# Gate/up chunks on 64-row halves, and the first numerators moved behind them, in a gated mix of linear attention and a gated feed-forward

## The chip, the cores and the metric

The kernel runs on one core of a Trainium2 chip. The metric is the device time of one execution in microseconds (us); the lower the better.

## The reference

A sequence of 2048 tokens of width 640 goes through two branches. Branch A is linear attention with 32 heads of 20 features, where the softmax of the projected features and of their negatives takes the place of the attention softmax. Branch B is a feed-forward block of width 1728 with a gelu gate. A sigmoid per token mixes them.

```python
g = sigmoid((x * gate_w).sum(-1, keepdims=True))
q, k, v = split_heads(x @ wqkv)                    # 32 heads of 20
phi = lambda z: concat([softmax(z @ w_phi), softmax(-(z @ w_phi))])
kv, z = phi(k).T @ v, phi(k).sum(tokens)           # per head
o = (phi(q) @ kv) / (phi(q) @ z + 1e-6)
a = merge_heads(o) @ wo
b = (gelu(x @ w_gate) * (x @ w_up)) @ w_down
out = g * a + (1 - g) * b
```

## The kernel before

The program is written by hand, and a small layer (`_Sched`) puts in the semaphore waits. Each operation names what it reads and writes, and a write waits for the last reader of each engine. The PSUM banks are named `("ps", 0)` to `("ps", 7)`; each holds 128 x 512 fp32 numbers. Operations run on each engine in the order in which the Python code issues them.

The stages in order:

- `attention_state`: the projections, the exponentials of keys and queries, and the sums over tokens (`gram`, L637) that become the small matrices `KV`. It ends about 80 us into the span.
- Gate/up, four blocks of 512 tokens (`gateups`). A block has 14 chunks of the width 1728, in the order 0, 1, 13, 2 to 12; chunk 13 is the narrow remainder. `gateup` issues for a chunk five full-height matmuls (128 rows, 512 columns, L464) for the gate into one bank and five for up into the next, then gelu on ScalarE (L779) from the gate bank, and the product with the up bank on VectorE (L781). The products stay in SBUF as `hT`. Chunks take turns on the bank pairs (0, 1) and (6, 7).
- Down, the same four blocks (`downs`). `down_pair` makes two tiles of 128 tokens: 64-row matmuls (L898), two at a time, one on the upper half of the rows into one tile's bank and one on the lower half into the other's; in the second half of the work ("closing") the halves change banks. Each `yield` of it is one such pair, called a step here; there are 148 in a block, 74 for each two tiles, of which 38 are opening. The last five of every pass multiply the attention output `goT` with `wo`. The banks are again (0, 1) and (6, 7).
- Between these, the attention output of each 128 tokens, called a numerator here (`num`, tile t = 0 to 15). `num_mms` issues 22 matmuls of 64 rows and 66 columns (L817), two at a time, into four banks: two for each of the two signs. `num_steps` issues eleven VectorE operations: a reciprocal from the banks (L851), seven more small ones, two wide multiplies from the banks (L863) to O1 and O2, and their sum (L866) to Og. A DMA transpose (L869, SP queue) brings Og to `goT`. All of VectorE's operations that read banks name all four of them.

In the down stage the numerators use banks 2 to 5, and their places are given in steps of the block:

```python
at = (1, 31, 61, 91)
for b in range(self.NB):
    downs(b, {at[k]: 4 * b + 2 + k for k in range(4 if b < 3 else 2)})
```

Numerators 0 and 1 are needed by the first two tiles of the down stage, and so come earlier: in block 1 of gate/up, behind its fifth chunk. `num_pair` issues their 44 matmuls in one go into banks 2 to 7, and `first_nums` deals out the VectorE steps between the products of the next chunks, which use other bank pairs meanwhile.

Of the kernel before, what the change touches and what calls it, by code (L numbers as in the profile page):

```python
# [3 lines left out]
P = 128  # L4
BF16 = mybir.dt.bfloat16
F32 = mybir.dt.float32
AF = mybir.ActivationFunctionType
ALU = mybir.AluOpType
# [99 lines left out]
class _Kernel:  # L108
    S, D, H, DH, F = 2048, 640, 32, 20, 1728
    KD = D // P  # L110
# [7 lines left out]
    DB = DH + 2  # L118
# [641 lines left out]
    def gateup(self, b, c, banks):  # L760
        sc = self.sc
        xs = lambda kt: self.xT[:, kt, b * self.BT:(b + 1) * self.BT]
        xr = [("xT", t) for t in range(4 * b, 4 * b + 4)]
        old = (self.oldw, self.oldk, self.oldq, [("xT", t) for t in range(12)])[b]
        hT, hk = self.hT(b, c), b
        slot = self.gn % 3
        self.gn += 1
        if c < 13:
            i = 0 if c < 7 else 1
            early = c in self.UP + self.LATE  # L770
            done = early and b == 0
            if done:
                banks = banks[::-1]
            for w, wk, bk in ((self.wg_sb, "wg", banks[0]), (self.wu_sb, "wu", banks[1]))[:1 if done else 2]:
                for kt in range(self.KD):
                    key = self.upheld(c)[1] if early and wk == "wu" else (wk, i, kt)
                    self.mm(bk, 0, 512, w[:, kt, c * P:(c + 1) * P], xs(kt), kt == 0, kt == self.KD - 1, xr + [key])
            up, upk = (self.upheld(c)[0], ("upf", c)) if done else (self.bank(banks[1]), ("ps", banks[1]))
            sc.op("act", lambda e: e.activation(self.gl[:, slot, :], self.bank(banks[0]), AF.Gelu_apprx_tanh),  # L779
                  reads=[("ps", banks[0])], writes=[("gl", slot)], guard=self.oldw)  # L780
            sc.op("dve", lambda e: e.tensor_tensor(hT, up, self.gl[:, slot, :], ALU.mult),  # L781
                  reads=[upk, ("gl", slot)], writes=[("hT", hk, c)], guard=old)
        else:
            bk = banks[0]
            for kt in range(self.KD):
                self.mm(bk, 0, 512, self.wgu_sb[:, kt, :], xs(kt), kt == 0, kt == self.KD - 1, xr + ["wgu0", "wgu1"])
            sc.op("act", lambda e: e.activation(self.gl[64:128, slot, :], self.ps[0:64, bk * 512:bk * 512 + 512],
                                                AF.Gelu_apprx_tanh),
                  reads=[("ps", bk)], writes=[("gl", slot)], guard=self.oldw)
            for r in (0, 1):  # L790
                odd = lambda v: v.rearrange("p (u r q) -> p u r q", r=2, q=P)[:, :, r, :]
                sc.op("dve", lambda e: e.tensor_tensor(
                    odd(hT[64 * r:64 * r + 64, :]), odd(self.ps[64:128, bk * 512:bk * 512 + 512]),
                    odd(self.gl[64:128, slot, :]), ALU.mult),
                    reads=[("ps", bk), ("gl", slot)], writes=[("hT", hk, c, r)], guard=old)

    def before_num(self):
        return ([("upf", c) for c in self.UP + self.LATE] + ["kstage", "qstage"] + [("wref", k, h) for k in (0, 3) for h in (0, self.HM)] + [("wref", k, 0) for k in (1, 2, 4)] + [("xtok", k) for k in range(4)] + ["wkT", "wqT"])

    def num(self, t):  # L800
        NBK, DB, old = self.NUMB, self.DB, self.before_num()
        w = self.HG * DB
        base = [(NBK + 2 * s) * 512 + 512 - 6 * w for s in (0, 1)]
        self.num_mms(t, base, 0)
        rb = [("ps", NBK + k) for k in range(4)]
        for step in self.num_steps(t, base, rb, old):
            step()

    def num_mms(self, t, base, late):
        sc, w = self.sc, self.HG * self.DB  # L810
        for g in range(self.G):
            n = min(w, self.H * self.DB - w * g)
            for s in (0, 1):
                a, o = 64 * s, base[s] + w * g
                edge = o // 512 != (o + w) // 512
                first = g == 0 or (o - w) // 512 != o // 512
                sc.op("pe", lambda e: e.matmul(  # L817
                    self.ps[:, o:o + n], self.Eq[a:a + 64, g, t * P:(t + 1) * P], self.KV[a:a + 64, g, 0:n],
                    start=first and not (late and g == 0), stop=edge or g == self.G - 1, skip_group_check=True),
                    reads=[("Eq", t), "KVd", ("KV", 0), ("KV", 8), ("KV", 10)], writes=[("ps", o // 512)],  # L820
                    signal=edge or g == self.G - 1)

    def num_pair(self):
        w = self.HG * self.DB
        top = 512 - 6 * w
        over = 512 + 512 - 3 * w
        bases = [[(2 + 3 * s) * 512 + c for s in (0, 1)] for c in (top, over)]
        rb = [("ps", b) for b in range(2, 8)]
        steps = []
        for t in (0, 1):  # L830
            self.num_mms(t, bases[t], t)
        for t in (0, 1):
            n = {0: (0, 1, 3, 4), 1: (1, 2, 4, 5)}[t]
            steps.append(self.num_steps(t, bases[t], [rb[k] for k in n], self.before_num()))
        return steps

    def num_steps(self, t, base, rb, old):
        sc = self.sc
        DB, DH, H = self.DB, self.DH, self.H
        sl = t % 2  # L840
# [2 lines left out]
        Dn = [v[:, :, DH + 1] for v in V]  # L843
        R = lambda k: self.RH[:, sl, k, :]
        key = lambda k: ("RH", sl, k)
        small, wide, fin = [], [], []
        into = small

        def dve(fn, reads, writes, guard=()):
            into.append(lambda: sc.op("dve", fn, reads=reads, writes=writes, guard=guard))  # L850
        dve(lambda e: e.reciprocal(R(0), Dn[1]), rb, [key(0)], guard=old)  # L851
        dve(lambda e: e.tensor_tensor(R(1), Dn[0], R(0), ALU.mult), rb + [key(0)], [key(1)])
        dve(lambda e: e.tensor_tensor(R(2), Z[1], R(1), ALU.mult), rb + [key(1)], [key(2)])
# [2 lines left out]
        dve(lambda e: e.reciprocal(R(5), R(4)), [key(4)], [key(5)])  # L856
        dve(lambda e: e.tensor_scalar(R(6), R(5), self.Gr[:, t:t + 1], None, op0=ALU.mult), [key(5), "Gr"], [key(6)])
        dve(lambda e: e.tensor_tensor(R(7), R(6), R(1), ALU.mult), [key(6), key(1)], [key(7)])
        into = wide
        for s, dst in ((0, self.O1), (1, self.O2)):  # L860
            o = dst[:, sl, :].rearrange("p (h d) -> p h d", d=DH)
            f = R(6 + s).unsqueeze(2).to_broadcast([P, H, DH])
            dve(lambda e, o=o, f=f, s=s: e.tensor_tensor(o, V[s][:, :, 0:DH], f, ALU.mult),  # L863
                rb + [key(6 + s)], [("O", s, sl)], guard=old)
        into = fin
        dve(lambda e: e.tensor_tensor(self.Og[:, sl, :], self.O1[:, sl, :], self.O2[:, sl, :], ALU.add),  # L866
            [("O", 0, sl), ("O", 1, sl)], [("Og", sl)], guard=old)
        gs = t % 8
        fin.append(lambda: sc.dma("sp", lambda e: e.dma_start_transpose(self.goT[:, gs, :, :], self.Og[:, sl, :]),  # L869
                                  reads=[("Og", sl)], writes=[("goT", gs)], guard=old))  # L870

        def run(part):
            for f in part:
                f()
        return [lambda p=p: run(p) for p in (small, wide, fin)]

    def down_pair(self, t0, banks, widths):

# [60 lines left out]
                    evac(h)  # L939
                yield None  # L940

    NUMB = 2
    oldk = [("Ek", k, s) for k in range(5) for s in (0, 1)] + [(w, k) for w in ("Ekc", "Ekp") for k in range(5)] + [
        (w, k) for w in ("vaug", "vmain", "vone") for k in range(9)]
    oldq = [("Eqt", k, s) for k in range(4) for s in (0, 1)] + [(w, k) for w in ("Eqtc", "Eqtp") for k in range(4)] + [
# [3 lines left out]
    def ffn(self):  # L949
        self.gn = 0  # L950
        self.pn = 0
        pairs = [(0, 1), (6, 7)]

        def gateups(b, after, other={}):
            for idx, c in enumerate([0, 1, 13] + list(range(2, 13))):
                self.gateup(b, c, other.get(idx, pairs[self.pn % 2]))
                self.pn += 1
                after(idx)

        def downs(b, side):  # L960
            p = [pairs[(self.pn + k) % 2] for k in (0, 1)]
            n = 0
            for t in (4 * b, 4 * b + 2):
                final = t + 2 == self.NT
                for _ in self.down_pair(t, p + [(2, 3)] if final else p, (256, 256, 128) if final else (320, 320)):
                    n += 1
                    if n in side:
                        self.num(side[n])

        def state(idx):  # L970
            if idx < 4:
                self.gram(12 + idx)
            if idx == 3:
                self.kv_state()
                self.gates()

        left = []

        def first_nums(idx):
            if idx == 4:  # L980
                left.extend(f for steps in self.num_pair() for f in steps)
            for _ in range({4: 1, 5: 1, 6: 2, 7: 1, 8: 1}.get(idx, 0)):
                left.pop(0)()

        def none(idx):
            pass
        at = (1, 31, 61, 91)
        gateups(0, state)
        gateups(1, first_nums, {k: ((0, 1), (0, 1), (0, 5), (1, 2))[k - 5 if k < 7 else 2 + (k - 7) % 2]
                                for k in range(5, 14)})  # L990
        gateups(2, none)
        gateups(3, none)
        for b in range(self.NB):
            downs(b, {at[k]: 4 * b + 2 + k for k in range(4 if b < 3 else 2)})

# [43 lines left out]
```

## Time and profile before

| What | Value |
|---|---|
| Time, median of 3 runs | 283.51 us (283.3 to 283.77) |
| Span of the profiled execution | 282.4 us |
| Around the span (median less span; the profiled execution has no other time of its own) | about 1.1 us |
| TensorE matmuls busy | 278.6 us, 99% |
| VectorE, ScalarE busy | 173.2 us (61%), 105.9 us (38%) |
| Granted TensorE clock | 1.000 |
| Gate/up blocks | about 80 to 194.8 us |
| Down stage | 194.8 to 280.4 us |

The span runs from the first to the last instruction. In the timeline a line gives the start, the busy time, the engine, the line of the program, the operation and its operands; a bracket gives the idle time before it and what ended it. PE is TensorE's matmuls, PEld its weight loads, DVE is VectorE, ACT ScalarE. [...]

### The profile page before, as it was taken

The page shows a single profiled execution, that of the slowest core. Times are in us where ns is not written, and L with a number is a line of the kernel's source. Part 1 is how long each engine was busy: PE and PEld are TensorE (multiplying, and loading weights), DVE is VectorE, ACT ScalarE, POOL GpSimd, SP SyncE. Part 2 cuts the span into 40 slices and gives each one's busy share as a digit, 9 for nine tenths or more (in the row PEclk, how much of TensorE's full clock was granted, in tenths as well). Part 3 has the DMA queues.
Part 4 walks back from the last instruction along what each step waited for, and adds up shares of the span by engine and source line. Part 5 has one row for each costly group of instructions (what it writes and reads, how often), then busy time and mean ns, then how long its engine had stood idle before and what let it go on. Part 6 is the DMA issues. An engine that isn't in the chain of part 4 may idle for free.

```text
span 282.4 us, 6904 instructions
## 1 busy us (share of the span) xinstructions
PE 278.6 (99%) x2926; PEld 168.6 (60%) x2926; DVE 173.2 (61%) x329; ACT 105.9 (38%) x204; POOL 15.1 (5%) x69
## 2 busy tenths in 40 slices
PE   7999999999999999999999999999999999999996
PEld 4566766665665444444444444445777777777786
DVE  1456999999997523694333324235883883883801
ACT  3246978777793332223232232321112112112011
POOL 7511001101000000000000000000000000000000
PEclk9999999999999999999999999999999999999999
DMA  7999169787789910011000000000133132532221
GB/s 213 193 223 190 29 127 172 153 175 149 157 175 274 350 51 0 2 24 23 2 0 0 0 2 0 0 0 2 26 50 98 46 49 78 66 49 73 73 72 49
DMA packets 60378, 24.11 MB, mean 85 GB/s; under 512 B 51002, under 2 KB 59834, under 8 KB 60346
## 3 DMA queue, kind: packets, MB, share of 16 engines
q1 hardware_dynamic: 59680, 23.63, 38.9%
q8 instruction: 23, 0.38, 0.6%
q10 hardware_dynamic: 666, 0.03, 0.2%
q14 instruction: 9, 0.07, 0.1%
HBM read 9.04 MB, written 2.62 MB: 41 GB/s over the span
## 4 chain that ended last, share of the span: by engine, by line
PE 97%; DMA 1%; SPq 0%; ACT 0%; issue 0%
PE ps L464 58%; PE ps L898 29%; PE ps L599 4%; PE ps L817 2%; PE ps L478 2%; PE ps L637 2%; DMA w<-in_A_wqkv_dram 1%; PE ps L404 1%; SPq L230 0%; SPq L251 0%; ACT outsb L911 0%; PE ps L370 0%
## 5 line engine op out<-in xcount | busy, mean ns | idle before, releaser
L464 PE MATMUL ps<-xT,wu_sb 128*128 128x512 bf16 x260 | 64.1, 379 | 0.0
L464 PE MATMUL ps<-xT,wg_sb 128*128 128x512 bf16 x260 | 63.9, 379 | 0.0
L779 ACT ACTIVATE gl<-ps 128x512 bf16<-128x512 f32 x52 | 31.0, 597 | 70.3 <-PE ps L464 70.3
L464 PE MATMUL ps<-w,xT 128*128 128x362 bf16 (+5 forms) x340 | 51.4, 302 | 0.0
L898 PE MATMUL ps<-wd_sb,hT 64*128 64x320 bf16 x648 | 48.4, 296 | 0.0
L781 DVE TENSOR_TENSOR hT<-ps,gl 128x512 bf16<-128x512 f32 x34 | 23.4, 689 | 37.7 <-PE ps L464 37.7
L464 PEld LDWEIGHTS ps<-xT,wu_sb 128*128 128x128 bf16 x260 | 25.4, 98 | 30.3 <-DVE hT L781 0.2
L464 PEld LDWEIGHTS ps<-xT,wg_sb 128*128 128x128 bf16 x260 | 25.1, 98 | 29.8 <-issue 0.2
L911 ACT ACTIVATE outsb<-ps,Gm 128x320 bf16<-128x320 f32 (+2 forms) x31 | 14.5, 515 | 71.8 <-PE ps L898 71.8
L464 PEld LDWEIGHTS ps<-w,xT 128*128 128x128 bf16 x340 | 31.9, 97 | 14.8
L898 PEld LDWEIGHTS ps<-wd_sb,hT 64*128 64x128 bf16 x648 | 30.9, 94 | 12.2 <-issue 0.4
L898 PE MATMUL ps<-wo_sb,goT 64*128 64x320 bf16 (+2 forms) x340 | 26.5, 288 | 0.0
L617 DVE TENSOR_REDUCE Dk<-Ek 128x66 f32<-128x1320 bf16 x16 | 24.3, 1520 | 2.3 <-ACT gcol L528 2.3
L626 DVE TENSOR_TENSOR Ek<-Ek,Dk 128x1320 bf16<-128x1320 bf16 x16 | 24.5, 1532 | 0.5
L863 DVE TENSOR_TENSOR O<-ps,RH 128x640 bf16<-128x640 f32 x32 | 24.7, 815 | 0.0
L538 ACT ACTIVATE Ek<-ps 128x627 bf16<-128x627 f32 x32 | 20.5, 693 | 6.4 <-PE ps L599 4.9
L538 ACT ACTIVATE Eqt<-ps 128x627 bf16<-128x627 f32 x32 | 20.6, 705 | 2.5 <-PE ps L464 2.5
L781 DVE TENSOR_TENSOR xT<-ps,gl 128x512 bf16<-128x512 f32 x13 | 9.0, 690 | 18.2 <-PE ps L464 18.2
L898 PEld LDWEIGHTS ps<-wo_sb,goT 64*128 64x128 bf16 x340 | 15.9, 94 | 5.3
L898 PE MATMUL ps<-wd_sb,xT 64*128 64x320 bf16 (+2 forms) x270 | 16.0, 269 | 0.0
L851 DVE RECIPROCAL RH<-ps 128x32 f32<-128x32 f32 x16 | 5.7, 357 | 14.4 <-PE ps L817 14.3
L898 PEld LDWEIGHTS ps<-wd_sb,xT 64*128 64x128 bf16 x270 | 12.1, 94 | 2.7
(90 smaller groups left out, 184.1 us busy)
## 6 DMA issues: line engine op xcount, KB each, us to landing
out_dram<-outsb SPq DMA_DIRECT2D x7, 320.0 KB, 2.3
wd_sb<-in_B_w_down_dram SPq DMA_DIRECT2D x1, 2080.0 KB, 11.0
wg_sb<-in_B_w_gate_dram SPq DMA_DIRECT2D x5, 224.0 KB, 3.1
wg_sb<-in_B_w_gate_dram SPq DMA_DIRECT2D x5, 192.0 KB, 3.5
wu_sb<-in_B_w_up_dram SPq DMA_DIRECT2D x5, 192.0 KB, 3.9
wo_sb<-in_A_wo_dram SPq DMA_DIRECT2D x1, 800.0 KB, 9.7
xtok<-in_A_x_dram SPq DMA_DIRECT2D x2, 320.0 KB, 3.3
w<-in_A_wqkv_dram SPq DMA_DIRECT2D x4, 160.0 KB, 4.0
```

The costliest lines, as they stand in the source:

```text
L464: self.sc.op("pe", lambda e: e.matmul(self.ps[:, bank * 512 + c0:bank * 512 + c0 + n], lhs, rhs, start=first, stop=fin), reads=reads, writ ...
L478: sc.op("pe", lambda e, c0=c0, n=n, bk=bk, col=col: e.matmul(self.bank(bk)[:, col:col + n], self.xT[:, kt, t * P:(t + 1) * P], self.w3[:, ...
L538: self.sc.op("act", lambda e: e.activation(dst, src, AF.Exp, scale=scale), reads=[("ps", b), ("ps", b + 1)], writes=[(name, sl, s)])
L599: self.sc.op("pe", lambda e: e.matmul(out, self.xT[:, kt, t * P:(t + 1) * P], self.w3[:, kt, c:c + 2 * n].rearrange("p (r w) -> p r w", w= ...
L617: self.sc.op("dve", lambda e: e.tensor_reduce(self.Dk[:, se, 0, :].rearrange("p (u h) -> p u h", h=self.HG), self.k_view(se), AX.X, ALU.ad ...
L626: sc.op("dve", lambda e: e.tensor_tensor(v, v, R.rearrange("p (u h) -> p u h", h=self.HG).unsqueeze(3).to_broadcast([P, 2 * self.G, self.H ...
L779: sc.op("act", lambda e: e.activation(self.gl[:, slot, :], self.bank(banks[0]), AF.Gelu_apprx_tanh), reads=[("ps", banks[0])], writes=[("g ...
L781: sc.op("dve", lambda e: e.tensor_tensor(hT, up, self.gl[:, slot, :], ALU.mult), reads=[upk, ("gl", slot)], writes=[("hT", hk, c)], guard=old)
L851: dve(lambda e: e.reciprocal(R(0), Dn[1]), rb, [key(0)], guard=old)
L863: dve(lambda e, o=o, f=f, s=s: e.tensor_tensor(o, V[s][:, :, 0:DH], f, ALU.mult), rb + [key(6 + s)], [("O", s, sl)], guard=old)
L898: sc.op("pe", lambda e: e.matmul(self.bank(bk, w), lhs, rhs, start=opens and x == 0, stop=end and not opens, skip_group_check=True), reads ...
L911: sc.op("act", lambda e: e.activation(dst, self.bank(bk, w), AF.Copy, scale=g), reads=rd, writes=wr)
```

## The change

Numerators 0 and 1 leave block 1, and with them `num_pair`, `first_nums` and the special bank pairs. Block 3 is issued by a new function, `last_gateups`. Its first six chunks run as before, but on the banks (2, 3) and (4, 5). Numerator 0 follows on banks 0, 1, 6, 7. The last eight chunks come in four groups of two, on the four banks (2 to 5), (0, 1, 6, 7), (0, 1, 6, 7), (2 to 5), with numerator 1 (banks 2 to 5) between the second and the third group. A group is issued by `gateup_halves`: for each chunk the upper 64 rows of the gate and, beside it, the lower 64 rows of up ("opening"), five pairs each; and then for each chunk the other halves ("closing"), with gate and up changing the halves of the rows. Gelu and product of a chunk follow its closing. In the down stage the places of the numerators change. The remaining numerators' operations are the same, and so is the number of gelu and product operations.

```diff
-            sc.op("act", lambda e: e.activation(self.gl[:, slot, :], self.bank(banks[0]), AF.Gelu_apprx_tanh),
...
+            self.gateup_evac(b, c, banks[0], slot, up, upk, old)
...
+    def gateup_halves(self, b, cs, pairs):
...
+        for close in (0, 1):
+            for c, banks in zip(cs, pairs):
+                i = 0 if c < 7 else 1
+                for kt in range(KD):
+                    for r in (0, 1):
+                        w, wk, bk = ((self.wg_sb, "wg", banks[0]), (self.wu_sb, "wu", banks[1]))[r ^ close]
...
+                        a, end = 64 * r, kt == KD - 1
+                        sc.op("pe", lambda e: e.matmul(
+                            self.bank(bk), w[a:a + 64, kt, c * P:(c + 1) * P],
+                            self.xT[a:a + 64, kt, b * self.BT:(b + 1) * self.BT], start=close == 0 and kt == 0,
+                            stop=close == 1 and end, skip_group_check=True),
...
+                            after=[("turn", bk)] if close and kt == 0 else ())
+                if close:
+                    slot = self.gn % 3
+                    self.gn += 1
+                    self.gateup_evac(b, c, banks[0], slot, self.bank(banks[1]), ("ps", banks[1]), old)
...
-    def num(self, t):
...
+    def num(self, t, banks=(2, 4)):
...
+        base = [b * 512 + 512 - 6 * w for b in banks]
+        self.num_mms(t, base)
+        rb = [("ps", b + k) for b in banks for k in (0, 1)]
+        self.num_steps(t, base, rb, old)
...
-    def num_pair(self):
...
-        def first_nums(idx):
-            if idx == 4:
-                left.extend(f for steps in self.num_pair() for f in steps)
-            for _ in range({4: 1, 5: 1, 6: 2, 7: 1, 8: 1}.get(idx, 0)):
-                left.pop(0)()
...
-        at = (1, 31, 61, 91)
+        def last_gateups(b):
+            middle, n = [(2, 3), (4, 5)], 6
+            for idx in range(n):
+                self.gateup(b, order[idx], middle[idx % 2])
+            self.num(0, (0, 6))
+            for g, banks in enumerate((middle, pairs, pairs, middle)):
+                if g == 2:
+                    self.num(1)
+                self.gateup_halves(b, order[n + 2 * g:n + 2 * g + 2], banks)
+        at = (12, 38, 64, 91)
...
-        gateups(1, first_nums, {k: ((0, 1), (0, 1), (0, 5), (1, 2))[k - 5 if k < 7 else 2 + (k - 7) % 2]
-                                for k in range(5, 14)})
+        gateups(1, none)
         gateups(2, none)
-        gateups(3, none)
+        last_gateups(3)
```

In the changed program the numerators' matmuls are at line 844, and the halves' at line 813.

More of the change, by code (lines that the diff above doesn't have):

```diff
@@ L778, in gateup @@
             up, upk = (self.upheld(c)[0], ("upf", c)) if done else (self.bank(banks[1]), ("ps", banks[1]))
[L779 to L782, printed above, removed]
+            self.gateup_evac(b, c, banks[0], slot, up, upk, old)
         else:
@@ L795, in gateup, with gateup_evac @@
                     reads=[("ps", bk), ("gl", slot)], writes=[("hT", hk, c, r)], guard=old)
+    def gateup_evac(self, b, c, bank, slot, up, upk, old):
+        sc, hT = self.sc, self.hT(b, c)
+        sc.op("act", lambda e: e.activation(self.gl[:, slot, :], self.bank(bank), AF.Gelu_apprx_tanh),
+              reads=[("ps", bank)], writes=[("gl", slot)], guard=self.oldw)
+        sc.op("dve", lambda e: e.tensor_tensor(hT, up, self.gl[:, slot, :], ALU.mult),
+              reads=[upk, ("gl", slot)], writes=[("hT", b, c)], guard=old)
@@ new lines, in gateup_halves @@
+    def gateup_halves(self, b, cs, pairs):
+        sc, KD = self.sc, self.KD
+        old = [("xT", t) for t in range(12)]
+        for close in (0, 1):
[4 more added lines that the diff above has]
+                        w, wk, bk = ((self.wg_sb, "wg", banks[0]), (self.wu_sb, "wu", banks[1]))[r ^ close]
+                        key = self.upheld(c)[1] if c in self.UP + self.LATE and wk == "wu" else (wk, i, kt)
+                        a, end = 64 * r, kt == KD - 1
[3 more added lines that the diff above has]
+                            stop=close == 1 and end, skip_group_check=True),
+                            reads=[("xT", t) for t in range(4 * b, 4 * b + 4)] + [key],
+                            writes=[("ps", bk)] + ([("turn", bk)] if end else []), signal=end,
+                            after=[("turn", bk)] if close and kt == 0 else ())
[3 more added lines that the diff above has]
+                    self.gateup_evac(b, c, banks[0], slot, self.bank(banks[1]), ("ps", banks[1]), old)
@@ L797, in before_num @@
     def before_num(self):
         return ([("upf", c) for c in self.UP + self.LATE] + ["kstage", "qstage"] + [("wref", k, h) for k in (0, 3) for h in (0, self.HM)] + [("wref", k, 0) for k in (1, 2, 4)] + [("xtok", k) for k in range(4)] + ["wkT", "wqT"])
-    def num(self, t):
[L801 to L807, printed above, removed]
@@ L809, in num_mms @@
-    def num_mms(self, t, base, late):
+    def num(self, t, banks=(2, 4)):
+        old = self.before_num()
+        w = self.HG * self.DB
+        base = [b * 512 + 512 - 6 * w for b in banks]
+        self.num_mms(t, base)
+        rb = [("ps", b + k) for b in banks for k in (0, 1)]
+        self.num_steps(t, base, rb, old)
+    def num_mms(self, t, base):
         sc, w = self.sc, self.HG * self.DB
@@ L818, in num_mms @@
                     self.ps[:, o:o + n], self.Eq[a:a + 64, g, t * P:(t + 1) * P], self.KV[a:a + 64, g, 0:n],
-                    start=first and not (late and g == 0), stop=edge or g == self.G - 1, skip_group_check=True),
+                    start=first, stop=edge or g == self.G - 1, skip_group_check=True),
                     reads=[("Eq", t), "KVd", ("KV", 0), ("KV", 8), ("KV", 10)], writes=[("ps", o // 512)],
                     signal=edge or g == self.G - 1)
-    def num_pair(self):
[L824 to L835, printed above, removed]
     def num_steps(self, t, base, rb, old):
@@ L845, in num_steps @@
         key = lambda k: ("RH", sl, k)
-        small, wide, fin = [], [], []
-        into = small
         def dve(fn, reads, writes, guard=()):
-            into.append(lambda: sc.op("dve", fn, reads=reads, writes=writes, guard=guard))
+            sc.op("dve", fn, reads=reads, writes=writes, guard=guard)
         dve(lambda e: e.reciprocal(R(0), Dn[1]), rb, [key(0)], guard=old)
@@ L858, in num_steps @@
         dve(lambda e: e.tensor_tensor(R(7), R(6), R(1), ALU.mult), [key(6), key(1)], [key(7)])
-        into = wide
         for s, dst in ((0, self.O1), (1, self.O2)):
@@ L864, in num_steps @@
                 rb + [key(6 + s)], [("O", s, sl)], guard=old)
-        into = fin
         dve(lambda e: e.tensor_tensor(self.Og[:, sl, :], self.O1[:, sl, :], self.O2[:, sl, :], ALU.add),
@@ L868, in num_steps @@
         gs = t % 8
[L869 to L875, printed above, removed]
+        sc.dma("sp", lambda e: e.dma_start_transpose(self.goT[:, gs, :, :], self.Og[:, sl, :]),
+               reads=[("Og", sl)], writes=[("goT", gs)], guard=old)
     def down_pair(self, t0, banks, widths):
@@ L940, in down_pair @@
                 yield None
-    NUMB = 2
     oldk = [("Ek", k, s) for k in range(5) for s in (0, 1)] + [(w, k) for w in ("Ekc", "Ekp") for k in range(5)] + [
@@ L952, in ffn, with gateups @@
         pairs = [(0, 1), (6, 7)]
-        def gateups(b, after, other={}):
-            for idx, c in enumerate([0, 1, 13] + list(range(2, 13))):
-                self.gateup(b, c, other.get(idx, pairs[self.pn % 2]))
+        order = [0, 1, 13] + list(range(2, 13))
+        def gateups(b, after):
+            for idx, c in enumerate(order):
+                self.gateup(b, c, pairs[self.pn % 2])
                 self.pn += 1
@@ L975, in state @@
                 self.gates()
-        left = []
-        def first_nums(idx):
-            if idx == 4:
-                left.extend(f for steps in self.num_pair() for f in steps)
-            for _ in range({4: 1, 5: 1, 6: 2, 7: 1, 8: 1}.get(idx, 0)):
-                left.pop(0)()
         def none(idx):
             pass
-        at = (1, 31, 61, 91)
+        def last_gateups(b):
[8 more added lines that the diff above has]
+        at = (12, 38, 64, 91)
         gateups(0, state)
-        gateups(1, first_nums, {k: ((0, 1), (0, 1), (0, 5), (1, 2))[k - 5 if k < 7 else 2 + (k - 7) % 2]
-                                for k in range(5, 14)})
+        gateups(1, none)
         gateups(2, none)
-        gateups(3, none)
+        last_gateups(3)
         for b in range(self.NB):
```

## The prediction

> **What bounds the kernel now.** I read the page's busy shares first, then the chain of waits in order of time, then the timeline of the two stages the change touches. The page:
>
> ```profile
> PE 278.6 (99%) x2926; PEld 168.6 (60%) x2926; DVE 173.2 (61%) x329; ACT 105.9 (38%) x204; POOL 15.1 (5%) x69
> PEclk9999999999999999999999999999999999999999
> ```
>
> TensorE has no slack and runs at the full granted clock all along, so every nanosecond that its stream loses or gains is a nanosecond of the span. The chain around the end of the gate/up blocks:
>
> ```profile
> 116.27 0.79 PE ps L817 x44
> 117.06 77.81 PE ps L464 x360
> 194.87 0.24 PE ps L898 x2
> 195.11 0.34 PE ps L817 x22
> 195.45 4.08 PE ps L898 x60
> 199.53 0.34 PE ps L817 x22
> ```
>
> Full-height matmuls of 512 columns follow each other at 77.81/360 = 216.1 ns. A step of the down projection (two 64-row matmuls of 320 columns side by side) takes 4.08/30 = 136 ns. A numerator takes 0.34 us between two such stretches of exactly 30 steps. So one numerator follows the last after 30 x 0.136 + 0.34 = 4.42 us, and nothing stalls at that distance. The timeline says how near it is to stalling:
>
> ```profile
> 203.52 0.10 PEld L898 LDWEIGHTS ps<-wd_sb,hT 64*128 64x128 bf16 x2
> 203.70 0.47 PEld L817 LDWEIGHTS ps<-KV,Eq 64*128 64x128 bf16 x22
> 203.79 0.50 PE L817 MATMUL ps<-KV,Eq 64*128 64x66 bf16 x22
> ...
> 204.45 0.36 DVE L851 RECIPROCAL RH<-ps 128x32 f32<-128x32 f32 x1 [0.22 <-PE ps L817]
> ...
> 206.52 1.55 DVE L863 TENSOR_TENSOR O<-ps,RH 128x640 bf16<-128x640 f32 x2
> 208.12 0.38 PEld L817 LDWEIGHTS ps<-KV,Eq 64*128 64x128 bf16 x15
> 208.15 0.49 DVE L866 TENSOR_TENSOR Og<-O,O 128x640 bf16<-128x640 bf16 x1
> 208.21 0.39 PE L817 MATMUL ps<-KV,Eq 64*128 64x66 bf16 x14
> ```
>
> A numerator's first matmul at 203.79 leads to its reciprocal at 204.45 and to the end of its second wide multiply at 206.52 + 1.55 = 208.07: 4.28 us. That multiply is the last reader of banks 2 to 5, which the next numerator overwrites. The next numerator's weight load starts at 208.12, 0.05 after it, and its matmul at 208.21. The load is held by VectorE: after the longer distance at a block's end it starts with the step before it, ahead of its own matmul by a whole step:
>
> ```profile
> 216.29 0.30 PE L898 MATMUL ps<-wd_sb,hT 64*128 64x320 bf16 x2
> 216.29 0.23 PEld L817 LDWEIGHTS ps<-KV,Eq 64*128 64x128 bf16 x4
> 216.43 0.20 PE L817 MATMUL ps<-KV,Eq 64*128 64x66 bf16 x2
> ```
>
> So 30 steps between numerators is where VectorE's chain just hides. The change shortens this.
>
> **Change, part 1: numerators in the down projections.** Places 1, 31, 61, 91 become 12, 38, 64, 91. Per block the distances 30, 30, 30 become 26, 26, 27 steps; block 3 has only the first two places, so 30 becomes 26. That makes seven distances of 26 and three of 27. TensorE alone would arrive after 4.42 - 4 x 0.136 = 3.88 us, or 4.01 for 27. Banks 2 to 5 are free only 4.28 + x after the previous numerator's first matmul, x being the time from VectorE's end to the matmul. No stalled case is in the trace, so x is bounded: 0.06 if the matmul starts with its load, 0.05 after VectorE, as load and matmul do at 194.80 after the switch below; 0.14 if the 208.07 to 208.21 above is already the least. The first row has an emptied array, in the second the matmul may just be keeping its cadence; I take 0.09. Stall at 26: 4.28 + 0.09 - 3.88 = 0.49 (0.46 to 0.54); at 27: 0.36 (0.33 to 0.41). Sum 7 x 0.49 + 3 x 0.36 = 4.5 us (4.2 to 5.0). Behind the waiting load stands all of TensorE's queue, and nothing gives the time back, as TensorE has no idle time elsewhere. The final add (0.49) ends 0.6 after the multiplies, before the next reciprocal can start, so VectorE adds no more.
>
> The distance from 91 to the next block's 12 is 69 steps: no wait. Place 12 instead of 1 is needed by the new last group: its second up bank is freed by a product that ends 0.20 + 0.60 + 0.10 + 0.69 = 1.59 us after the group's last matmuls (the wait for gelu, gelu, the wait between, the product: durations as in the rows below, 0.10 from another chunk, where a gelu from 111.99 to 112.58 lets VectorE start at 112.68). With x it is 1.68; 12 steps are 1.63, and the numerator touches that bank only after its sixth pair, 0.2 later: no stall.
>
> **Part 2: fewer changes of array shape.** Every change between 128-row and 64-row matmuls costs time:
>
> ```profile
> 193.63 1.24 PE L464 MATMUL ps<-xT,wu_sb 128*128 128x512 bf16 x5
> 193.83 0.60 ACT L779 ACTIVATE gl<-ps 128x512 bf16<-128x512 f32 x1 [1.56 <-PE ps L464]
> 194.80 0.10 PEld L898 LDWEIGHTS ps<-wd_sb,hT 64*128 64x128 bf16 x2 [0.42 <-issue]
> 194.80 0.31 PE L898 MATMUL ps<-wd_sb,hT 64*128 64x320 bf16 x2
> ...
> 194.91 0.69 DVE L781 TENSOR_TENSOR xT<-ps,gl 128x512 bf16<-128x512 f32 x1 [1.47 <-PE ps L464]
> ```
>
> The fifth full matmul starts at 193.63 + 4 x 0.216 = 194.49 and the first half at 194.80: 0.31 in place of 0.216, so 0.10. Before there are three: into the numerators of block 1 (116.21), out of them (117.00, about 0.10 by the same reckoning) and into the down projections. After there is one, at the sixth chunk of block 3. Gain 0.20 us.
>
> **Part 3: eight chunks on halves.** 80 full matmuls become 80 pairs of halves. From 216.1 (512 columns) and 136 (320, a pair of halves): 0.417 ns per column, 2.5 fixed in both; a pair of 512 costs 216.1. Sum 0, from -0.2 (no fixed part) to +0.3 (the halves' offset of some 3 ns not hidden). The Trainium skill ("TensorE: Matmul & The Clock Gate", Measured speedup vs the span model) speaks against halves: side-by-side tiles take one matmul's duration and about 4 ns per further tile. By that page's figure 80 pairs would cost an estimated 0.3 us more and the sum would be 5.3; the 136 ns step shows no such tail. A closing half waits for the other row group's opening of its bank, which lies one chunk's opening (1.08 us) back; the down projections do the same at a smaller distance without a stall.
>
> **Part 4: waits in block 3.** Zero is numerator 0's first matmul; it takes 0.35, a pass over a chunk (five pairs) 1.08, a group of two chunks 4.32. Numerator 0 uses banks 0, 1, 6, 7, needed again at 4.67. VectorE first does the sixth chunk's product, as at 194.91; the trace has the next reciprocal behind that product at 195.62, 1.13 after the last full matmul's start, which here is -0.31. The chain from reciprocal to second multiply is 208.07 - 204.45 = 3.62, so it ends at 1.13 - 0.31 + 3.62 = 4.44, plus x = 4.53: no stall, 0.14 to spare. Group 2 ends at 9.0, numerator 1 at 9.34 (its banks were freed at 6.4). Group 3 reuses at once the banks of group 2; now gate and up finish together at a chunk's end, so gelu no longer runs under the up matmuls: the first chunk's product ends at 7.91 + 1.59 = 9.50 and, plus x, holds the up half to 9.59. The second product ends at 8.99 + 1.59 = 10.58; numerator 1's chain stands behind it on VectorE and ends at 10.58 + 0.02 + 3.62 = 14.22. Group 4 opens on its banks at 14.31 instead of 9.34 + 4.32 = 13.66. The first stall (0.25) is inside this: 0.65 us in all (0.62 to 0.70).
>
> **Part 5: nothing.** The two transposes to goT that leave block 1 for block 3 sit on an SP queue that is empty there (2.6 us to landing). Numerator 1's sum is done at 14.8, landed at 17.4; group 4 ends at 18.6 and goT is first read 28 steps later. ScalarE and VectorE have the same instructions, so leaving block 1 frees nothing on the path: TensorE's 216 ns hold through it.
>
> Sum: 4.5 - 0.2 + 0 + 0.65 = +5.0 us (4.7 to 5.5). The span would be 282.4 + 5.0 = 287.4; about 1.1 us lies between the profile's span and the median 283.51, and I leave it unchanged: 288.5.
>
> **Rivals.** *No stall between numerators (0.06)*, the other side: the held load would be only a late prefetch and the multiply's end no bound, or VectorE's chain shorter than 3.88. Place: the ten distances; it decides from 0.4 us less in the chain. For it: no stall is in the trace. Against: the load follows the multiply by 0.05 whenever the distance is 30 and not at a block's end. Then +0.45 with the waits of block 3, 284.0; without them too -0.2, 283.3: about the same time, not slower by more than 0.2%.
>
> *Each stall also pays a restart (0.06)*: a held load meets an emptied array, as at a change of shape, 0.10 more for each of 12 stalls: +6.2, 289.7. Against it: the change of shape is a different cause.
>
> *The clock drops (0.02)*: ten gaps of half a microsecond could lower the granted clock. If each stretch of 3.54 us after a stall ran at half pace: 10 x 3.5 = +35, 324 us. Against: PEclk stays at 9 through the 0.4 us wait for a DMA near 6 us. The Trainium skill ("TensorE: Matmul & The Clock Gate", A second HAM failure mode: psum-queue depth-cycling) tells of such micro-idling between groups.
>
> *The halves stream faster (0.01)* and the stalls are absent: 80 x 10 ns = 0.8 less, 282.5.
>
> **Numbers.** The forecast has 0.85. About 0.2% (0.57 us) can be told from no change. Slower by more takes the forecast, the restart and the clock: 0.93; same takes the first rival: 0.05; faster the last and the spread of the first: 0.02. The range joins the sum's ends (288.2, 289.0), the halves' bounds, the spread of the runs (0.25) and the restart's value: 287.7 to 289.7.
>
> **What would show it.** Right: ten weight loads of L844 that follow the second wide multiply by 0.05 with TensorE idle 0.3 to 0.5 before their matmuls; numerators 4.3 to 4.4 us apart; one gap of 0.31 before numerator 0 and none before the down projections; a stall of some 0.25 at group 3 and 0.4 at group 4; PEclk at 9. Wrong: numerators at 3.9 us, pairs of 512 columns off 216 ns, or a gap at the second group.

## The result

| | Before | Changed |
|---|---|---|
| Median | 283.51 us | 288.04 us (287.85 to 288.47, 5 runs) |
| Ratio to before | | 1.0168, interval 1.0156 to 1.0179 |
| Span of the profiled execution | 282.4 us | 287.2 us |

The changed kernel is slower by 1.7%, 4.4 to 5.1 us by the interval. The forecast was 288.5 us, in a range from 287.7 to 289.7.

### The profile page after: what moved, and what is told of

The parts are those of the page before. It is cut to its first block, busy times and chain, and to the rows that moved or that the text cites. A ratio compares the mean times of both kernels' runs of the same rounds, so it can differ in the third digit from the quotient of the medians.

```text
span 287.2 us, 7052 instructions
## 1 busy us (share of the span) xinstructions
PE 280.8 (98%) x2994; PEld 168.7 (59%) x3006; DVE 173.3 (60%) x329; ACT 106.0 (37%) x204; POOL 15.2 (5%) x69
## 5 line engine op out<-in xcount | busy, mean ns | idle before, releaser
L464 PE MATMUL ps<-xT,wu_sb 128*128 128x512 bf16 x214 | 52.9, 379 | 0.3
L464 PE MATMUL ps<-xT,wg_sb 128*128 128x512 bf16 x214 | 52.7, 379 | 0.3
L464 PE MATMUL ps<-w,xT 128*128 128x362 bf16 (+5 forms) x340 | 51.4, 302 | 0.0
L464 PEld LDWEIGHTS ps<-w,xT 128*128 128x128 bf16 x340 | 31.9, 97 | 14.8
L464 PEld LDWEIGHTS ps<-xT,wu_sb 128*128 128x128 bf16 x220 | 21.5, 98 | 25.6
L464 PEld LDWEIGHTS ps<-xT,wg_sb 128*128 128x128 bf16 x220 | 21.1, 98 | 25.4 <-ACT gl L796 0.4
L902 PE MATMUL ps<-wo_sb,goT 64*128 64x320 bf16 (+2 forms) x340 | 25.8, 288 | 0.0
L873 DVE TENSOR_TENSOR O<-ps,RH 128x640 bf16<-128x640 f32 x32 | 24.7, 814 | 0.0
L813 PE MATMUL ps<-xT,wg_sb 64*128 64x512 bf16 x80 | 18.0, 376 | 0.1
L813 PE MATMUL ps<-xT,wu_sb 64*128 64x512 bf16 x80 | 17.5, 376 | 0.0
```

The costliest lines, as they stand in the source:

```text
L464: self.sc.op("pe", lambda e: e.matmul(self.ps[:, bank * 512 + c0:bank * 512 + c0 + n], lhs, rhs, start=first, stop=fin), reads=reads, writ ...
L813: sc.op("pe", lambda e: e.matmul(self.bank(bk), w[a:a + 64, kt, c * P:(c + 1) * P], self.xT[a:a + 64, kt, b * self.BT:(b + 1) * self.BT], ...
L902: sc.op("pe", lambda e: e.matmul(self.bank(bk, w), lhs, rhs, start=opens and x == 0, stop=end and not opens, skip_group_check=True), reads ...
```

## The profile after

TensorE is still the bound (busy 98% of the span, 99% before), and the granted clock is 1.000 as it was. The page, busy time with its share of the span, and the granted clock by core:

```profile
PE 280.8 (98%) x2994; PEld 168.7 (59%) x3006; DVE 173.3 (60%) x329; ACT 106.0 (37%) x204; POOL 15.2 (5%) x69
...
core 0: 287.2 us, clock 1.000
```

VectorE's busy time is the same (173.2 before). The waits of the weight loads, as total, times and longest, name what is new:

```profile
PEld ps L844 <- DVE O L873: 5.9, 10, 0.6
...
PEld ps L813 <- DVE O L873: 0.6, 1, 0.6
...
PEld ps L813 <- DVE xT L798: 0.5, 2, 0.3
...
PEld ps L464 <- ACT gl L796: 0.4, 1, 0.4
```

Ten numerators wait for a wide multiply (L873): the ten distances of 26 and 27. The two lines of L813 are the waits of block 3, and the line of L464 is one in block 2 that is taken up below. These times are the idle time of the weight loads' queue, which starts earlier than the idle time of the matmuls. The recorded durations of matmuls overlap (0.37 us for a half of 512 columns at a pace of 0.216 us), so the loss itself is read from the starts of the matmuls. The timeline of the first two numerators of the down stage:

```profile
196.89 0.50 PE L844 MATMUL ps<-KV,Eq 64*128 64x66 bf16 x22
...
197.56 0.36 DVE L862 RECIPROCAL RH<-ps 128x32 f32<-128x32 f32 x1 [0.68 <-PE ps L844]
...
199.63 1.54 DVE L873 TENSOR_TENSOR O<-ps,RH 128x640 bf16<-128x640 f32 x2
201.23 0.40 PEld L844 LDWEIGHTS ps<-KV,Eq 64*128 64x128 bf16 x22 [0.63 <-DVE O L873]
201.23 0.52 PE L844 MATMUL ps<-KV,Eq 64*128 64x66 bf16 x22 [0.30 <-DVE O L873]
...
205.58 0.40 PEld L844 LDWEIGHTS ps<-KV,Eq 64*128 64x128 bf16 x22 [0.63 <-DVE O L873]
```

The chain from 196.89 to the second multiply's end at 199.63 + 1.54 = 201.17 is the 4.28 us of before. The weight load follows 0.06 later, as it did. But TensorE now has nothing left to do while it waits, and the matmul starts together with the load. From numerator to numerator (201.23 to 205.58) it is 4.35 us where 26 steps and a numerator would need 3.88. From the step before to the numerator, the starts of the matmuls are 0.600 us apart at a distance of 26 and 0.464 at one of 27, in place of 0.136: 0.464 us lost at each distance of 26 and 0.328 at each of 27.

The chain of numerator 1 and the opening of groups 3 and 4 in block 3:

```profile
185.59 0.69 DVE L798 TENSOR_TENSOR xT<-ps,gl 128x512 bf16<-128x512 f32 x1 [2.54 <-ACT gl L796]
186.67 0.69 DVE L798 TENSOR_TENSOR xT<-ps,gl 128x512 bf16<-128x512 f32 x1 [0.39 <-ACT gl L796]
187.28 0.35 DVE L862 RECIPROCAL RH<-ps 128x32 f32<-128x32 f32 x1
...
189.33 1.55 DVE L873 TENSOR_TENSOR O<-ps,RH 128x640 bf16<-128x640 f32 x2
```

```profile
186.09 0.37 PE L813 MATMUL ps<-xT,wg_sb 64*128 64x512 bf16 x1
186.33 0.09 PEld L813 LDWEIGHTS ps<-xT,wu_sb 64*128 64x128 bf16 x1 [0.18 <-DVE xT L798]
...
190.45 0.87 PE L813 MATMUL ps<-xT,wg_sb 64*128 64x512 bf16 x2
...
190.93 0.09 PEld L813 LDWEIGHTS ps<-xT,wg_sb 64*128 64x128 bf16 x1 [0.60 <-DVE O L873]
```

Group 3's gate half starts at 186.09, its up half only after the product that ends at 185.59 + 0.69 = 186.28: 0.25 us. Group 4 waits for numerator 1's multiplies, which end at 190.88; the matmul before starts at 190.45, the next at 190.935, where 0.216 is the pace: another 0.27. Group 2 shows no gap.

One more wait is new, and it lies outside the stages of the change, in block 2 of gate/up, where VectorE's product of the narrow chunk 13 comes late:

```profile
141.12 0.59 ACT L784 ACTIVATE gl<-ps 64x512 bf16<-64x512 f32 x1 [1.56 <-PE ps L464]
...
142.17 0.89 DVE L789 TENSOR_TENSOR hT<-ps,gl 64x256 bf16<-64x256 f32 x2 [1.44 <-PE ps L464]
...
143.17 0.78 PEld L464 LDWEIGHTS ps<-xT,wg_sb 128*128 128x128 bf16 x5 [0.42 <-ACT gl L796]
143.20 1.24 PE L464 MATMUL ps<-xT,wg_sb 128*128 128x512 bf16 x5
```

The product starts 0.46 us after its gelu; in the other blocks, and in all four blocks before, it is 0.10. The matmuls of the next chunk but one write its bank and start at 143.20, 0.12 us behind their pace. The view names ScalarE for this wait, but the product is the reader that ends last (143.06). The four runs below that are edits of the changed kernel have the same wait, and the gap grows with the lateness: 337 ns between two matmuls where the product is 458 ns behind its gelu, 348 where it is 469.

## The experiments

**Distances of 30 again**, in the changed kernel.

```diff
-        at = (12, 38, 64, 91)
+        at = (12, 42, 72, 102)
```

> The changed kernel with the numerators of the down stage at 12, 42, 72, 102: thirty steps apart again, all else as changed. My theory (VectorE's chain from a numerator's first matmul to its second wide multiply, 4.28 us and 0.06 to the next load, outlasts 26 or 27 steps): the ten stalls, 4.3 us in the changed kernel's trace, vanish; what is left is the two bank waits of block 3 (0.54) less two changes of array shape (0.20): 283.5 + 0.34 = 283.85 us, no gap in TensorE's stream after 191 us. The rival (the loss lies in the halves or in the numerators' new place in block 3): stays near 288.0.

Measured 283.66 us, ratio 1.0007 (0.9998 to 1.0016), beside 283.57 for the kernel before on the same chip. Of 4.5 us nearly all is back, and no numerator of the down stage waits:

```profile
201.10 0.47 PEld L844 LDWEIGHTS ps<-KV,Eq 64*128 64x128 bf16 x22
...
201.19 0.48 PE L844 MATMUL ps<-KV,Eq 64*128 64x66 bf16 x20
```

Load and matmul stand 0.09 apart again, as before the change. The two waits of block 3 are still in the trace, at the same size (0.25 and 0.28), and so is the one in block 2 (0.12). With the saved 0.20 these are 0.45 us, the upper end of the interval; the times, 0.1 apart, do not resolve them.

**The distances alone**, in the kernel before.

```diff
-        at = (1, 31, 61, 91)
+        at = (12, 38, 64, 91)
```

> The kernel before with one edit: numerators of the down stage at 12, 38, 64, 91. My theory: seven stalls of 0.47 and three of 0.33, and 0.01 for each restart: 283.5 + 4.4 = 287.9 us. The rival (the halves carry the loss): 283.5. A third, that the stalls come only with numerators 0 and 1 in block 3, because VectorE is behind there: also 283.5.

Measured 287.78 us, ratio 1.0153 (1.0140 to 1.0166), with the changed kernel's line of waits:

```profile
PEld ps L817 <- DVE O L863: 5.9, 10, 0.6
```

So the stalls need neither the halves nor numerators 0 and 1 in block 3. This one line of the change costs 4.2 us alone, beside 4.5 for the whole.

**The halves alone**, in the kernel before. Numerators 0 and 1 stay in block 1; those of the down stage start at step 12 in place of 1, thirty steps apart as before.

```diff
+    def gateup_halves(self, b, cs, pairs):
...
-        at = (1, 31, 61, 91)
+        at = (12, 42, 72, 102)
...
-        gateups(3, none)
+        order, middle = [0, 1, 13] + list(range(2, 13)), [(2, 3), (4, 5)]
+        for idx in range(6):
+            self.gateup(3, order[idx], middle[idx % 2])
+        for g, banks in enumerate((pairs, middle, pairs, middle)):
+            self.gateup_halves(3, order[6 + 2 * g:8 + 2 * g], banks)
...
```

> The kernel before with only the last eight chunks of block 3 on halves, groups of two on alternating sets of four banks; numerators 0 and 1 stay in block 1, those of the down stage at 12, 42, 72, 102. My theory: 80 pairs of 512 columns take what 80 full matmuls took (216 ns), there are three changes of array shape as before, and no bank wait in block 3: 283.5 us, within 0.2. A rival (a second tile costs 4 ns per pair): 283.8. A second (closing halves wait for the opening of the other row group): 0.16 for each of eight chunks, 284.8.

Measured 283.18 us, ratio 0.9996 (0.9988 to 1.0005): the same time as before. The chain of waits in order of time has the 160 halves in one piece:

```profile
177.65 17.37 PE ps L816 x160
195.02 1.63 PE ps L929 x24
```

17.37/80 = 217 ns for a pair of 512 columns, with the rest of the one change of shape in it; the starts inside are 216 ns apart. No closing waits for its turn, and with alternating sets of banks no group waits for a product. So the halves cost nothing that can be told. This kernel leaves out both things that block 3's waits are put down to, the reuse of banks at once (group 3) and numerator 1 among the groups (group 4); which belongs to which is read from the waits, and a later run bears it out.

**Distances of 28**, in the changed kernel.

```diff
-        at = (12, 38, 64, 91)
+        at = (12, 40, 68, 96)
```

> The changed kernel with the numerators of the down stage at 12, 40, 68, 96: ten distances of 28. My theory, in which a stall is the part of VectorE's 4.34 us that the steps leave uncovered: 4.34 - (4.42 - 2 x 0.136) = 0.19 each, 1.9 and 0.1 for the restarts: 283.85 + 2.0 = 285.8 us. The rival (each stall has a fixed price of some 0.45, whatever the distance): 288.3. If VectorE's chain were no cause: 288.0 as changed or 283.85.

Measured 285.60 us, ratio 1.0080 (1.0067 to 1.0093). Ten gaps of 0.33 us in place of 0.136: 0.19 each, what was expected of an uncovered rest, and far from a fixed price. The numerators again follow each other in 4.35 us:

```profile
200.67 0.51 PE L844 MATMUL ps<-KV,Eq 64*128 64x66 bf16 x22
...
205.02 0.46 PE L844 MATMUL ps<-KV,Eq 64*128 64x66 bf16 x18
```

**A shorter chain on VectorE**, distances of 26 and 27.

```diff
-        dve(lambda e: e.tensor_scalar(R(6), R(5), self.Gr[:, t:t + 1], None, op0=ALU.mult), [key(5), "Gr"], [key(6)])
-        dve(lambda e: e.tensor_tensor(R(7), R(6), R(1), ALU.mult), [key(6), key(1)], [key(7)])
+        dve(lambda e: e.tensor_tensor(R(7), R(5), R(1), ALU.mult), [key(5), key(1)], [key(7)])
...
-            dve(lambda e, o=o, f=f, s=s: e.tensor_tensor(o, V[s][:, :, 0:DH], f, ALU.mult),
+            dve(lambda e, o=o, f=f, s=s: e.scalar_tensor_tensor(
+                o, V[s][:, :, 0:DH], self.Gr[:, t:t + 1], f, ALU.mult, ALU.mult),
...
```

> The changed kernel, distances of 26 and 27 as changed, with VectorE's chain one operation shorter: the factor Gr is taken into the two wide multiplies (one instruction each, as before) instead of an own operation on 32 columns, which takes 0.27 us from start to start. If the wide multiplies keep their 0.81 us, my theory has the chain at 4.28 - 0.27 + 0.06 = 4.07 us from matmul to matmul: stalls of 0.19 (seven) and 0.06 (three) instead of 0.47 and 0.33, together 1.5, 0.1 for restarts; the wait before group 4, which ends on numerator 1's chain, goes from 0.28 to about 0, the one in group 3 (0.25) stays, as it ends on a product: 283.5 - 0.2 + 0.26 + 1.6 = 285.2 us. The rival (the distances cost by themselves, by what TensorE does in them): 288.0 less 0 to 0.3.

Measured 287.10 us, ratio 1.0132 (1.0117 to 1.0148): the expectation missed by 1.9 us. Its "if" did not hold. The wide multiply with the third operand takes longer:

```profile
L872 DVE SCALAR_TENSOR_TENSOR O<-ps,Gr,RH 128x640 bf16<-128x640 f32 x28 | 23.4, 875 | 0.0
```

That is 875 ns in place of 814, twice, so the chain is shorter by 0.155 us and not by 0.27. With that the trace is largely accounted for: numerators follow in 4.196 us (4.35 - 0.155), the stalls are 0.31 at 26 and 0.18 at 27, together 2.7 in place of 4.2, and group 4's gap is 0.334 in place of 0.485, shorter by the same 0.15; so that wait does end on numerator 1's chain. Group 3's gap (0.253) did not move, as it ends on a product. One reciprocal came 0.35 us late:

```profile
219.63 0.36 DVE L862 RECIPROCAL RH<-ps 128x32 f32<-128x32 f32 x1 [6.03 <-PE ps L844]
...
223.15 0.40 PEld L844 LDWEIGHTS ps<-KV,Eq 64*128 64x128 bf16 x22 [0.83 <-DVE O L872]
```

It starts 1.02 us after its numerator's first matmul, where the others take 0.67 to 0.68, and the next numerator's stall is longer by as much, on top of the 2.7. The next run has it at the same numerator (the seventh), the other kernels don't. It is as late as the product in block 2, and the places fit a pattern: counted with its sequencer's entries in the trace, the product is VectorE's 192nd and this reciprocal its 320th, 128 apart. Why is open.

With this, the restarts (0.1), block 3 (0.25 and 0.12), block 2 (0.12) and the saved changes of shape (0.2), the terms make 3.4 us, where this run's span is 3.5 longer than the median span of the kernel before on the same chip, and the times differ by 3.8. The last 0.3 lies around the span and is not explained.

**The shorter chain with distances of 28.**

> The same shorter chain with the distances of 28 (12, 40, 68, 96), where the longer chain cost 2.0 us. My theory: 4.07 is less than 28 steps and a numerator (4.15), so no stall between numerators; 283.5 - 0.2 + 0.26 = 283.6 us. The rival (distances by themselves): 285.6, as with the longer chain.

Measured 284.41 us, ratio 1.0044 (1.0030 to 1.0058): off by 0.8 in the same way. With the chain's 4.196 us as measured, 28 steps (4.147) leave 0.04 at each of ten numerators, 0.4 together. The one late reciprocal adds 0.35, restarts 0.1, block 3 0.25 + 0.12, block 2 0.12, and the saved changes of shape take 0.2: 283.26 + 1.1 = 284.4 (283.26 is the kernel before on the same chip).

The four kernels in a table, times from the starts of the numerators' matmuls; the first distance of a block is 0.01 us less, and the one behind the late reciprocal is left out:

| Chain | Distance 26 | Distance 28 |
|---|---|---|
| as changed | 4.350 us apart | 4.350 us apart |
| one operation less | 4.196 us apart | 4.196 us apart |
| TensorE's own need | 3.88 us | 4.15 us |

In these kernels the spacing does not depend on the distance as long as it is too short; it follows the chain.

No kernel here beats the one before. What the change could save is the 0.2 us of two changes of array shape, 0.07%, less than the measurement tells apart; the kernel with distances of 30 has that saving and by its trace pays it back in blocks 2 and 3.

## Why the prediction was right

- **Distances (4.5 us forecast, 4.2 and 0.1 measured).** Seven stalls of 0.464 and three of 0.328 are 4.23 us, at the lower bound of 4.2. The term that was a little too large is x, taken as 0.09: it is 0.057 in every stall of the changed kernel, so the matmul starts with the held load, as after a change of shape, and the 0.14 of before was only the matmul keeping its cadence. Behind each stall the second pair of the numerator comes 0.01 late, and the stream with it: the 0.1. The forecast's sum had no such term; its rival had 0.10 for each stall.
- **Changes of array shape (-0.2).** One gap of 0.312 before numerator 0, none before the down stage, as forecast. The experiments do not resolve 0.2 us in time.
- **Halves (0).** Shown alone: 216 ns a pair. The Trainium skill's 4 ns for a second tile ("TensorE: Matmul & The Clock Gate", Measured speedup vs the span model) does not add up in this stream: by that figure 80 pairs would have taken an estimated 0.3 us more than they did.
- **Block 3 (0.65, measured 0.25 + 0.27).** Below its own bounds of 0.62 to 0.70. The first wait is right. The second was mis-sized: the reciprocal of numerator 1 starts at 187.28, 0.08 before the recorded end of the product ahead of it (186.67 + 0.69), where the sum had 0.02 after it, and x was 0.03 less. The 0.02 was a misreading: it was taken from the reciprocal at 195.62, which was waiting for its own numerator's matmuls (they start at 194.95, and 0.67 later is the usual place of that reciprocal) and not for the product ahead.
- **Block 2 (0 forecast, 0.12 measured).** Here the forecast missed a term: it said that leaving block 1 frees nothing on the path and that the pace of 216 ns holds through it. The late product of chunk 13 breaks it once. In the kernel before, VectorE's 192nd entry is another product, in block 1 behind the numerators' steps. It is late too (it starts at 124.92, 0.24 after VectorE fell idle, and its gelu had ended at 123.20), but no matmul waits for it.
- **Rivals.** No stall between numerators: refuted by the ten waits, and by 287.78 from the places alone. A restart price of 0.10: it is 0.01. The clock: 1.000. Halves that stream faster: 216 ns a pair. The Trainium skill's lowering of the clock by micro-idling (the same page, A second HAM failure mode: psum-queue depth-cycling) did not come here with ten waits that cost up to 0.46 us, each followed by 3.9 us or more of dense work.

The terms as measured are 4.23 + 0.1 - 0.2 + 0.52 + 0.12 = 4.8, beside 4.8 between the two profiled spans and 4.5 between the medians. The forecast's 5.0 came this near in part by luck: the stalls and block 3 were 0.4 too large together, and 0.2 was missing for the restarts and block 2. Its sum also has a slip, as the lower end is 4.2 - 0.2 + 0.62 = 4.6 and not 4.7. The median's 4.5 lies just under either, inside the range but not inside the ends of the sum.

## What to carry to other kernels

When a full engine hands a buffer to another engine and wants it back, compare the round trip (here 0.67 + 3.61 + 0.06 us) with the work placed between two uses, step by step: a distance that just hides it looks free in the profile. Here the sign that it was the limit was a weight load that started 0.05 us behind the other engine's end instead of running ahead with the step before. Below that distance each use here cost the missing work in full, at once, and the spacing was set by the other engine's chain alone. An operation folded into a wider one shortens a chain only by what the wider one does not grow.

## What the runs showed of the hardware

- A stalled weight load lets its matmul start with it: 0.057 us from the recorded end of the VectorE operation to the matmul, in all ten stalls of the changed kernel (0.055 to 0.058 in the others), with about 0.01 us lost again in the pair that follows.
- A VectorE multiply of 128 x 640 from PSUM takes 875 ns with a per-row factor as third operand and 814 ns without; on 32 columns the form with a third operand, there a constant, took 191 ns, as the plain one did.
- A VectorE operation can start 0.08 us before the recorded end of the one ahead of it, where it does not read that one's result (187.28 behind a product that ends at 187.36).
- Two 64-row matmuls of 512 columns side by side take 216 ns a pair in a stream, the pace of one full-height matmul.
- A VectorE operation behind a wait can start 0.35 us late at a fixed place of its list: the 192nd entry in all eight traces (by 0.2 in the three kernels with numerators in block 1), and the 320th in the two with the shorter chain. The first cost TensorE 0.12 us in the changed kernel, the second 0.35 in those two. The cause is open.
